# RWKV-5 attention followed by an MLP mixer on one core: the last batch's k read by one transfer instead of six

## The chip, the core and the metric

The kernel runs on one core of a Trainium2 chip. A core has five engines with instruction queues of their own: PE (TensorE, matrix products), DVE (VectorE), ACT (ScalarE), POOL (GpSimd) and SP (SyncE, which here issues most of the transfers between HBM and the core's SBUF). Each engine works its queue strictly in the written order; engines wait for each other and for transfers through semaphores. The metric is the device time of one launch in microseconds (us).

## The reference

Inputs r, k, v are (4, 8, 768, 48): four batches, eight heads, 768 steps, 48 channels, in float32; w and u are (8, 48). The attention's output, with the heads side by side, is the input x (4, 768, 384) of the mixer.

```python
for t in range(S):                                     # attention, per batch and head
    cur = einsum('bhd,bhe->bhde', u * k[t], v[t])
    y[t] = einsum('bhd,bhde->bhe', r[t], state + cur)
    state = w * state + einsum('bhd,bhe->bhde', k[t], v[t])

h  = relu(x.transpose(0, 2, 1) @ w_tok1) @ w_tok2      # mixer: along the 768 steps, 256 hidden
u  = x + h.transpose(0, 2, 1)
h2 = relu(u @ w_ch1) @ w_ch2                           # along the 384 channels, 1536 hidden
return u + h2
```

## The kernel before

**Tiling.** Each batch is cut into six chunks of 128 steps, with the steps on the 128 partitions and 8 heads x 48 channels in the free dimension. The recurrence is done chunk by chunk: inside a chunk as masked scores (`at_ps`, then `AT`) times v, between chunks by a state of 48 x 48 per head (`kv_ps`, then `S`). Decays are factors w to the power of a step number; they are kept in tables (`wnat`, `wp`, `wpair`) and multiplied onto k and r (`kr`).

**One chunk of the last two batches.** k, r and v of the chunk come by three loads on SP (tiles `kt`, `rt`, `vt`, 192 KB each; for every partition 8 pieces of 192 bytes). For these batches POOL makes all products (`POOL_ONLY`, line 193): `ku` = k times u, `rku` = `ku` times r, and `kr`, whose halves are k and r with their decays. DVE sums `rku` per head to `adg`. ACT turns v into bf16, `vb` (line 819). POOL makes `yd` from `vb` and `adg`. SP sends `kr` through a transposing transfer (`rk<-kr`, line 881). PE then multiplies the scores, for two chunks in one step (`GROUPS`, line 204; `scores`, line 972); DVE masks them; PE makes y and the state; DVE adds `yd` and writes `x_b`.

**The mixer of a batch** (line 1096 and after) starts when its six chunks of `x_b` are there: `h1_ps` and `hT_ps` along the steps, `z_ps` up to the hidden channels, a relu by ACT or DVE (`zr`), `h_ps` down to the output, and the stores (`out_dram<-osb`). Its matmuls are put between those of the next batches' attention, so that at about 85 to 110 us the last batch's attention shares all engines with the mixers of the batches before.

**The order** is not left to a scheduler: `ORDER` (line 21) lists all tasks in the sequence in which they are emitted, which fixes each engine's queue. `BUFS` (line 66) lists for every pool which buffer each tile takes; the PSUM banks of the pool `m` are handed round by it, and a matmul that starts a new tile waits until the bank's former contents have been read. `HOLD` and `GATES` (lines 174 and 187) let some early loads, and a few later ones, wait for the one before or for a weight's transfer. Of the last batch's loads of k, the one of chunk 1 has a gate.

**SP's queue around the change**, by the written order: k of chunk 0 of the last batch, v, r, k, a store, r, k, v, v, r, a transpose of `kr`, a store, k, a transpose, a transpose of `u_sb` (the mixer's `uT`), k, another of these, r, k, and on with transposes, r and v. Every transfer on SP uses one of eight semaphores in turn, and so also waits for the transfer eight places before it.

**ACT's queue there**: copies of a state (`S<-kv_ps`), the cast of v for a chunk of the last batch, two relus `zr<-z_ps` of the mixer of batch 1, a relu of `h1_ps` of batch 2, two more casts of v.

**Constants.** `mask2`, `place` and the table `wn2` serve a variant that handles chunks in pairs (`pairs`); the list `PAIRED` (line 196) is empty, so nothing reads them. `warm` is a tile of zeros that PE multiplies to fill its time at the start and at a few places of the first batch.

The profile writes L294 for nearly all instructions: this is the line of the wrapper that keeps them in program order. Tiles' names tell them apart.

Of the kernel before, what the change touches and what calls it, by code (L numbers as in the profile page):

```python
# [11 lines left out]
f32 = mybir.dt.float32  # L12
bf16 = mybir.dt.bfloat16
i32 = mybir.dt.int32
ACTF = mybir.ActivationFunctionType
ALU = mybir.AluOpType
# [203 lines left out]
class Plan:  # L220
# [10 lines left out]
    def add(self, engine, kind, emit, deps=(), take=(), use=()):  # L231
        self.tasks.append((emit, [d for d in deps if d is not None]))
        return len(self.tasks) - 1
# [22 lines left out]
def kernel(  # L256
# [14 lines left out]
    B, H, S, D = r.shape  # L271
    dm = H * D
    T = 128
    C = S // T
    NG = 3
    HP = H // 2
    P = 64
# [5 lines left out]
    const = ctx.enter_context(tc.tile_pool(name="const", bufs=1))  # L283
# [12 lines left out]
    pe, dve, act, pool, sp = (InOrder(e) for e in (nc.tensor, nc.vector, nc.scalar, nc.gpsimd, nc.sync))  # L296
# [20 lines left out]
    def mul(on, out, a, c):  # L317
        engine_of[on].tensor_mul(out, a, c)
# [6 lines left out]
    PRODUCT = {"POOL": "mul2_POOL", "DVE": "mul2_DVE"}  # L325

    def h3(t):
        return t.rearrange("p (h d) -> p h d", h=H)

    def row(src):  # L330
# [6 lines left out]
    krs = [const.tile([128, 2, H, P], bf16, name=f"kr{i}") for i in range(NKP)]  # L337
    ones = const.tile([1, 128], f32, name="ones")
    u_bc = const.tile([128, dm], f32, name="u_bc")
    warm = const.tile([128, 512], bf16, name="warm")  # L340
    NW = C // 2
    iota_i = const.tile([128, 4 + 2 + 2 * NG], i32, name="iota_i")
    iota = const.tile([128, 4 + 2 + 2 * NG], f32, name="iota")
    ident_f = const.tile([128, 128], f32, name="ident_f")
    ident = const.tile([128, 128], bf16, name="ident")
    mask = const.tile([128, 128], f32, name="mask")
    mask2 = const.tile([128, 2, 128], f32, name="mask2")
    place = const.tile([128, 2, 128], bf16, name="place")
    lnw = const.tile([128, dm], f32, name="lnw")
    wn = {g: const.tile([128, g, dm], f32, name=f"wnat{g}") for g in (2, NG)}  # L350
    wp = const.tile([128, NG, dm], f32, name="wp")
# [3 lines left out]
    u_heads = wp[0:H, 2, 2 * P:4 * P]  # L355
    lnwd = const.tile([128, HP], f32, name="lnwd")
    wp2 = const.tile([128, 2, dm], f32, name="wpair")
    wn2 = const.tile([128, 2, dm], f32, name="wnpair")
    u_blk = const.tile([128, HP, H], bf16, name="u_blk")
    wG = {g: const.tile([128, HP], f32, name=f"wG{g}") for g in (2, NG)}  # L360
    bm = const.tile([128, HP, 2, D], f32, name="bm")
    wGm = {g: const.tile([128, HP, 2, D], f32, name=f"wGm{g}") for g in (2, NG)}
    S0s = [const.tile([128, HP, 2, D], bf16, name=f"S0_{i}") for i in range(2)]
    x_bs = [const.tile([128, C, dm], bf16, name=f"x_b{i}") for i in range(2)]
    wtok1 = wts.tile([128, C, dtok], bf16, name="wtok1")
    wtok2 = wts.tile([128, 2, S], bf16, name="wtok2")
    wch1 = [wts.tile([128, 3, n], bf16, name=f"wch1_{i}") for i, n in enumerate((PART * 128, dch - PART * 128))]
# [2 lines left out]
    def once(engine, kind, f, deps=(), **kw):  # L370
        return add(engine, kind, f, deps, **kw)
# [39 lines left out]
    t_mask = once("POOL", "mask", make_mask)  # L411

    def make_mask2():
        pool.memset(mask2, 1.0)
        for q in range(2):
            rows = mask2[q * P:(q + 1) * P]
            pool.affine_select(out=rows, in_=rows, compare_op=ALU.is_gt, fill=0.0, base=0, pattern=[[-1, 2], [1, 128]],
                               channel_multiplier=-2)

    t_mask2 = once("POOL", "mask2", make_mask2)  # L420

    def make_place():
        dve.memset(place, 0.0)
        for q in range(2):
            rows = slice(q * P, (q + 1) * P)
            for j in range(2):
                dve.tensor_copy(place[rows, j, j::2], ident[rows, rows])

    t_place = once("DVE", "place", make_place, [t_id])

# [25 lines left out]
    def decay(t, g, col, deps):  # L456
        return once("ACT", "act384s", lambda: act.activation(t[:, g, :], lnw, Exp, scale=iota[:, col:col + 1]),
                    [t_lnw] + deps)

    t_wn2 = [decay(wn2, j, j, [t_io2]) for j in range(2)]  # L460
    t_wp2 = [decay(wp2, j, 2 + j, [t_io2]) for j in range(2)]
    t_wn = {2: [decay(wn[2], g, 4 + g, [t_io]) for g in range(2)], NG: [decay(wn[NG], g, 6 + g, [t_io]) for g in range(NG)]}
    t_wG = {g: once("ACT", "ln_s", lambda g=g: act.activation(wG[g], lnwd, Exp, scale=float(g * T)), [t_lnwd])
# [45 lines left out]
    def load(b, c, i):  # L509
        nm, src = (("kt", k), ("rt", r), ("vt", v))[i]  # L510
        win = two_steps(b, c, i)
        nm = "win" if win else nm

        def f():
            if win:
                t = sb("win", [128, H, 2 * D], f32)
                dst = t
                what = src[b, :, ds(c * T, 2 * T), :].rearrange("h (p j) d -> p h (j d)", j=2)
            else:
                t = sb(nm, [128, dm], f32)  # L520
                dst = h3(t)
                what = src[b, :, ts(c, T), :].rearrange("h s d -> s h d")
            asked[b, c, i] = sp.dma_start(dst, what)
            loaded[b, c, i] = t
            if (b, c, i) in GATES:
                after(asked[b, c, i], sent[GATES[b, c, i]])
            if (b, c, i) in HOLD:
                after(asked[b, c, i], asked[HOLD[b, c, i]])

        return add("SP", "load2" if win else "load", f, [], take=(nm,))  # L530

    for b in range(B):
        for c in range(C):
# [266 lines left out]
    def unit(b, c):  # L800
# [3 lines left out]
        L = {}  # L804
# [21 lines left out]
        if first:  # L826
            def turn_k():
                L["trk"] = ps("trk", [128, HP, T], bf16)
                for a in range(HP):
                    pe.transpose(L["trk"][:, a, :], pair(L["kr"][:, 0], a), ident)  # L830

            def evac_k(on):
                L["ka"] = sb("rka", [128, HP, T], bf16)
                copy(on, L["ka"], L["trk"])

            def product(on):
                L["pr"] = sb("pr", [128, HP, T], bf16)
                mul(on, L["pr"], L["trk"] if on == "DVE" else L["ka"], rT())

            def sum_m():  # L840
                L["ad_ps"] = ps("ad_ps", [128, H])
                for a in range(HP):
                    pe.matmul(L["ad_ps"], L["pr"][:, a, :], u_blk[:, a, :], start=(a == 0), stop=(a == HP - 1))

            def copy_ad(on):
                L["adg"] = sb("adg", [128, H], f32)
                copy(on, L["adg"], L["ad_ps"])

            t_tk = add("PE", "tk", turn_k, [t_kp, t_id], take=("m",), use=[(t_kp, "kp")])
            t_ek = flex({"ACT": "copy512", "DVE": "copy512d"}, evac_k, [t_tk], take=("rka",), use=[(t_tk, "m")])  # L850
            use_k, use_r = [(t_ek, "rka")], [(W["t"], "rkb")]
            turned = [t_ek, W["t"]]
            kT = lambda: L["ka"]
            rT = lambda: W["ra"][:, :, c % 2, :]
            t_pr = flex({"POOL": "prod_POOL", "DVE": "prod_DVE"}, product, turned, take=("pr",),
                        use=use_k + use_r + [(t_tk, "m")])
            t_sm = add("PE", "sm", sum_m, [t_pr, t_ublk], take=("m",), use=[(t_pr, "pr")])
            t_ad = flex({"ACT": "copy_ad", "DVE": "copy_ad"}, copy_ad, [t_sm], take=("adg",), use=[(t_sm, "m")])
        else:
            def mul_u(on):  # L860
                L["ku"] = sb("ku", [128, dm], f32)
                mul(on, L["ku"], loaded[b, c, 0], u_bc)

            def mul_rku(on):
                L["rku"] = sb("rku", [128, dm], f32)
                mul(on, L["rku"], L["ku"], loaded[b, c, 1])

            def sum_rku():
                L["adg"] = sb("adg", [128, H], f32)
                dve.tensor_reduce(L["adg"], h3(L["rku"]), axis=mybir.AxisListType.X, op=ALU.add)  # L870

            t_ku = flex(products, mul_u, [lk, t_ubc], take=("ku",), use=[(lk, "kt")])
            t_rku = flex(products, mul_rku, [t_ku, lr], take=("rku",), use=[(t_ku, "ku"), (lr, "rt")])
            t_ad = add("DVE", "sum384", sum_rku, [t_rku], take=("adg",), use=[(t_rku, "rku")])

            def mul_r(on):
                mul(on, L["kr"][:, 1, :, 0:D], h3(loaded[b, c, 1]), h3(wp[:, g, :]))

            t_rp = flex(products, mul_r, [lr, t_wp[g], t_kp], use=[(lr, "rt"), (t_kp, "kp")])
            if STYLE[n][0] == "dma":  # L880
                def turn_rk():
                    L["rk"] = sb("rk", [128, 2, HP, T], bf16)
                    sp.dma_start_transpose(L["rk"].rearrange("p j a s -> p (j a) s"),
                                           L["kr"].rearrange("p j h d -> p (j h d)"))

                t_ev = add("SP", "turn_rk", turn_rk, [t_kp, t_rp], take=("rk",), use=[(t_kp, "kp")])
            else:
                def turn_all():
                    L["tr"] = ps("tr_ps", [128, 2, HP, T], bf16)
                    for j in range(2):  # L890
                        for a in range(HP):
                            pe.transpose(L["tr"][:, j, a, :], pair(L["kr"][:, j], a), ident)

                def evac(on):
                    L["rk"] = sb("rk", [128, 2, HP, T], bf16)
                    copy(on, L["rk"], L["tr"])

                t_tr = add("PE", "tr_all", turn_all, [t_kp, t_rp, t_id], take=("m",), use=[(t_kp, "kp")])
                t_ev = flex({"ACT": "copy1024", "DVE": "copy1024d"}, evac, [t_tr], take=("rk",), use=[(t_tr, "m")])
            turned = [t_ev]  # L900
            use_k, use_r = [(t_ev, "rk")], [(t_ev, "rk")]
            kT = lambda: L["rk"][:, 0]
            rT = lambda: L["rk"][:, 1]
# [321 lines left out]
```

## Time and profile before

| what | value |
|---|---|
| time, median of 3 runs | 164.7 us (163.48 to 165.5) |
| profiled execution: span from its first to its last instruction | 160.1 us |
| profiled execution: its own whole time | not given by the page |
| granted clock of PE over the span | 1.000 |
| PE busy | 153.4 us, 96% |
| DVE / POOL / ACT busy | 111.6 / 88.8 / 68.2 us |
| read from HBM / written to it | 20.46 / 4.72 MB |

The page names instructions by engine, operation and tiles (`out<-in`). In a timeline a row is: start, duration, engine, operation, tiles, how many in a row, and in brackets the idle time of the engine before it and what ended that. `SPq` marks the issue of a transfer on SP; the transfer itself lands later. In a table of windows a row is: stretch, its length, then busy time (with the number of instructions) of PE, PE's weight loads, DVE, ACT and POOL, then PE's granted clock, the share of time that the transfer engines were busy, and GB/s. A row of waits is: who waited, for whom, us in total, how often, the longest. A row of transfers is: tiles, queue, kind, count, size, median us from issue to landing.

### The profile page before, as it was taken

The numbers are of one execution on the slowest core, as the hardware profiler recorded it, in microseconds if no ns is written. First come the engines' busy times: TensorE is split into PE (matmuls) and PEld (weight loads), VectorE is DVE, ScalarE is ACT, GpSimd is POOL, SyncE is SP. The second block draws the span as 40 slices with busy tenths as digits, with TensorE's granted clock in tenths as the row PEclk, the third lists the DMA queues.
The fourth block names the chain that finished last, engine by engine and source line by source line (L and its number), as shares of the span: only waits on it lengthen the run. The fifth ranks groups of instructions, "written<-read, shape, count | busy, mean of one in ns | idle before, by whom it ended". The sixth has DMA issues, their size and how long they took to land.

```text
span 160.1 us, 3797 instructions
## 1 busy us (share of the span) xinstructions
PE 153.4 (96%) x1463; PEld 102.6 (64%) x1463; DVE 111.6 (70%) x237; ACT 68.2 (43%) x150; POOL 88.8 (55%) x112
## 2 busy tenths in 40 slices
PE   6998799899999999999999999999999999999992
PEld 1464577567677677666767666677676556676572
DVE  6689884875697578397969939788997357422432
ACT  3999875438924254254524431144214102355000
POOL 7149991028179999899982997999822000000000
DMA  5999999999999979999999999999791064300222
GB/s 130 208 208 182 147 236 220 207 230 212 186 203 204 196 164 186 220 215 150 246 205 207 213 211 161 197 232 205 120 265 57 0 158 161 74 6 0 98 98 98
DMA packets 93061, 26.89 MB, mean 168 GB/s; under 512 B 87794, under 2 KB 92148, under 8 KB 93044
## 3 DMA queue, kind: packets, MB, share of 16 engines
q1 hardware_dynamic: 90688, 23.40, 72.6%
q0 software_dynamic: 2160, 3.15, 11.5%
q8 instruction: 11, 0.18, 0.5%
q10 hardware_dynamic: 196, 0.11, 0.2%
q14 instruction: 6, 0.05, 0.1%
HBM read 20.46 MB, written 4.72 MB: 157 GB/s over the span
## 4 chain that ended last, share of the span: by engine, by line
PE 76%; DMA 17%; ACT 2%; POOL 1%; issue 1%; SPq 1%; DVE 0%; POOLq 0%
PE h_ps L294 34%; PE z_ps L294 27%; DMA wch<-in_moe_w_ch_dram 7%; DMA kt<-in_k_dram 5%; DMA vt<-in_v_dram 5%; PE y_ps L294 4%; PE at_ps L294 3%; PE hT_ps L294 3%; PE kv_ps L294 2%; PE hx_ps L294 1%; PE trk L294 1%; ACT vb L294 1%; SPq L294 1%; PE tr_ps L294 1%; ACT x_b L294 1%
## 5 line engine op out<-in xcount | busy, mean ns | idle before, releaser
L294 PE MATMUL h_ps<-wch,zr 128*128 128x384 bf16 (+1 forms) x300 | 53.9, 320 | 0.0
L294 PE MATMUL z_ps<-uT,wch 128*128 128x384 bf16 x288 | 52.5, 327 | 0.6 <-DMA wch<-in_moe_w_ch_dram 0.6
L294 ACT ACTIVATE zr<-z_ps 128x384 bf16<-128x384 f32 x56 | 27.1, 492 | 39.5 <-PE z_ps L294 39.3
L294 PEld LDWEIGHTS <-wch 128*128 128x128 bf16 x288 | 31.1, 115 | 13.4 <-DMA wch<-in_moe_w_ch_dram 1.2
L294 PEld LDWEIGHTS <-zr 128*128 128x128 bf16 x300 | 27.6, 98 | 15.3
L294 DVE TENSOR_TENSOR AT<-at_ps,mask 128x512 bf16<-128x512 f32 x48 | 31.0, 683 | 3.7 <-PE at_ps L294 3.6
L294 DVE TENSOR_SCALAR zr<-z_ps 128x384 bf16<-128x384 f32 x40 | 21.4, 554 | 11.4 <-PE z_ps L294 8.6
L294 POOL TENSOR_TENSOR yd<-vb,adg 128x384 f32<-128x384 bf16 x18 | 14.8, 828 | 11.6 <-ACT vb L294 4.3
L294 POOL TENSOR_TENSOR kr<-kt,wnat 128x384 bf16<-128x384 f32 x19 | 19.3, 1019 | 3.0 <-DMA kt<-in_k_dram 2.9
L294 ACT CAST vb<-vt 128x384 bf16<-128x384 f32 x22 | 11.0, 511 | 12.6 <-DMA vt<-in_v_dram 12.6
L294 DVE TENSOR_TENSOR osb<-u_sb,h_ps 128x384 f32<-128x384 bf16 (+1 forms) x16 | 8.4, 528 | 9.9 <-PE h_ps L294 9.4
L294 PEld LDWEIGHTS <-kr 128*128 128x128 bf16 x176 | 11.8, 102 | 4.9 <-POOL kr L294 1.5
L294 POOL TENSOR_TENSOR ku<-kt,u_bc 128x384 f32<-128x384 f32 x12 | 12.1, 1008 | 0.5 <-DMA kt<-in_k_dram 0.5
L294 POOL TENSOR_TENSOR rku<-ku,rt 128x384 f32<-128x384 f32 x12 | 11.9, 1001 | 0.2
L294 POOL TENSOR_TENSOR kr<-rt,wp 128x384 bf16<-128x384 f32 x12 | 12.0, 1000 | 0.0
L294 PEld LDWEIGHTS <-wtok 128*128 128x128 bf16 x78 | 7.4, 98 | 4.4
L294 DVE TENSOR_TENSOR x_b<-y_ps,yd 128x384 bf16<-128x384 f32 x18 | 9.6, 549 | 0.6 <-PE y_ps L294 0.5
L294 PE MATMUL h_ps<-x_b,wtok 128*128 128x384 bf16 x48 | 8.8, 327 | 0.0
L294 PE MATMUL y_ps<-vb,AT 128*128 128x48 bf16 x192 | 8.7, 184 | 0.0
L294 ACT CAST S<-kv_ps 48x192 bf16<-48x192 f32 x18 | 5.6, 311 | 7.3 <-PE kv_ps L294 4.2
L294 POOL TENSOR_TENSOR pr<-rka,rkb 128x512 bf16<-128x512 bf16 x2 | 2.3, 1149 | 10.7 <-DVE rka L294 10.7
L294 DVE TENSOR_TENSOR u_sb<-x_b,hT_ps 128x384 bf16<-128x384 bf16 x15 | 7.6, 548 | 0.6 <-PE hT_ps L294 0.6
(93 smaller groups left out, 183.1 us busy)
## 6 DMA issues: line engine op xcount, KB each, us to landing
kt<-in_k_dram SPq DMA_DIRECT2D x24, 192.0 KB, 4.2
vt<-in_v_dram SPq DMA_DIRECT2D x24, 192.0 KB, 4.8
out_dram<-osb SPq DMA_DIRECT2D x23, 192.0 KB, 1.9
win<-in_r_dram SPq DMA_DIRECT2D x6, 384.0 KB, 4.9
rt<-in_r_dram SPq DMA_DIRECT2D x12, 192.0 KB, 3.2
wch<-in_moe_w_ch_dram POOLq DMA_DIRECT2D x4, 384.0 KB, 6.6
wtok<-in_moe_w_tok_dram POOLq DMA_DIRECT2D x2, 384.0 KB, 6.4
wch<-in_moe_w_ch_dram POOLq DMA_DIRECT2D x1, 768.0 KB, 11.3
```

The source lines that it names most:

```text
L294: return lambda *args, **kw: tc.keep_in_program_order(f(*args, **kw))
```

## The change

The six loads of k for batch 3 become one load of the whole slice k[3] into a tile of its own, `kw`, at the place where chunk 0's load was issued; the tasks of the other five issue nothing, and each chunk reads its part of `kw` (eight pieces of 48 values, 1152 bytes apart). The `kt` buffers and the gate of chunk 1's k are no longer used for this batch. `ku` is computed over the same 384 values in a shape with three dimensions.

Beside this, `mask2`, `place`, and the table `wn2` are no longer built, and `warm` becomes a view of the first part of `x_b1`, the mixer input of batches 1 and 3. In the queues, POOL loses a memset and two selects, DVE a memset and four small copies, ACT two exponentials, SP five loads. The order of everything else on every engine stays as it was; some waits name another of the eight semaphores, because the turn of SP's transfers has shifted.

```diff
     def h3(t):
+        if len(t.shape) == 3:
+            return t
         return t.rearrange("p (h d) -> p h d", h=H)
...
-    warm = const.tile([128, 512], bf16, name="warm")
...
-    mask2 = const.tile([128, 2, 128], f32, name="mask2")
-    place = const.tile([128, 2, 128], bf16, name="place")
...
-    wn2 = const.tile([128, 2, dm], f32, name="wnpair")
...
+    warm = x_bs[1][:, 0:2, :].rearrange("p c d -> p (c d)")[:, 0:512]
+    whole = const.tile([128, H * C, D], f32, name="kw")
...
     def make_mask2():
-        pool.memset(mask2, 1.0)
-        for q in range(2):
-            rows = mask2[q * P:(q + 1) * P]
-            pool.affine_select(out=rows, in_=rows, compare_op=ALU.is_gt, ...)
+        pass
...
     def make_place():
-        dve.memset(place, 0.0)
-        for q in range(2):
-            rows = slice(q * P, (q + 1) * P)
-            for j in range(2):
-                dve.tensor_copy(place[rows, j, j::2], ident[rows, rows])
+        pass
...
-    t_wn2 = [decay(wn2, j, j, [t_io2]) for j in range(2)]
+    t_wn2 = [once("ACT", "act384s", lambda: None, [t_lnw, t_io2]) for j in range(2)]
...
         def f():
+            if (b, i) == (3, 0):
+                if c == 0:
+                    asked[b, 0, 0] = sp.dma_start(whole, k[b].rearrange("h (c p) d -> p (h c) d", p=T))
+                asked[b, c, i] = asked[b, 0, 0]
+                loaded[b, c, i] = whole.rearrange("p (h c) d -> p h c d", c=C)[:, :, c, :]
+                return
             if win:
                 t = sb("win", [128, H, 2 * D], f32)
...
-        return add("SP", "load2" if win else "load", f, [], take=(nm,))
+        return add("SP", "load2" if win else "load", f, [])
...
             def mul_u(on):
                 L["ku"] = sb("ku", [128, dm], f32)
-                mul(on, L["ku"], loaded[b, c, 0], u_bc)
+                mul(on, h3(L["ku"]), h3(loaded[b, c, 0]), h3(u_bc))
```

More of the change, by code (lines that the diff above doesn't have):

```diff
@@ L413, in make_mask2 @@
     def make_mask2():
-        pool.memset(mask2, 1.0)
-        for q in range(2):
-            rows = mask2[q * P:(q + 1) * P]
-            pool.affine_select(out=rows, in_=rows, compare_op=ALU.is_gt, fill=0.0, base=0, pattern=[[-1, 2], [1, 128]],
-                               channel_multiplier=-2)
+        pass
     t_mask2 = once("POOL", "mask2", make_mask2)
     def make_place():
-        dve.memset(place, 0.0)
-        for q in range(2):
-            rows = slice(q * P, (q + 1) * P)
-            for j in range(2):
-                dve.tensor_copy(place[rows, j, j::2], ident[rows, rows])
+        pass
     t_place = once("DVE", "place", make_place, [t_id])
```

## The prediction

> **What bounds the kernel now.** I read the page's busy shares first, then the busy time of the stretch from 35 to 157 us, then what TensorE (PE) waited for in the whole span.
>
> ```profile
> span 160.1 us, 3797 instructions
> PE 153.4 (96%) x1463; PEld 102.6 (64%) x1463; DVE 111.6 (70%) x237; ACT 68.2 (43%) x150; POOL 88.8 (55%) x112
> ...
> GB/s 130 208 208 182 147 236 220 207 230 212 186 203 204 196 164 186 220 215 150 246 205 207 213 211 161 197 232 205 120 265 57 0 158 161 74 6 0 98 98 98
> ...
> 35.00:157.00 122.00, 121.86 (x1144) 83.28 (x1144) 83.66 (x165) 44.56 (x98) 70.96 (x77) 1.00 0.81 161
> ...
> PE kv_ps L294 <- DVE warm L294: 1.3, 1, 1.3
> PE trk L294 <- POOL kr L294: 0.6, 2, 0.5
> PE z_ps L294 <- DMA wch<-in_moe_w_ch_dram: 0.6, 2, 0.5
> ```
>
> From 35 us on PE is busy for 121.86 of 122.00 us: nothing else bounds that stretch, and nothing can be gained in it. But nothing is spare there either: a microsecond in which PE has to wait is a microsecond on the end. PE's own waits, of which these are the three longest, lie before that and sum to little. So the change is worth what it saves before 35 us less what it makes PE wait after that. The second thing to see is the row of GB/s: from 85 to 108 us about 205 GB/s are moved with hardly a break, so whatever is put in front of a transfer there delays it by its bytes.
>
> **The change, part by part.** Five of the six k loads of the last batch leave the sync queue, and the first becomes six times as large at the same place.
>
> ```profile
> 83.30 0.44 SPq L294 DMA_DIRECT2D kt<-in_k_dram  x1
> 83.84 0.65 SPq L294 DMA_DIRECT2D vt<-in_v_dram  x1
> 84.54 1.15 SPq L294 DMA_DIRECT2D rt<-in_r_dram  x1
> 85.74 0.70 SPq L294 DMA_DIRECT2D kt<-in_k_dram  x1
> ...
> 102.56 0.58 SPq L294 DMA_DIRECT2D kt<-in_k_dram  x1
> ...
> kt<-in_k_dram SPq DMA_DIRECT2D x24, 192.0 KB, 4.2
> ...
> 84.00:88.00 4.00, 4.00 (x66) 3.07 (x65) 4.00 (x8) 1.72 (x4) 1.03 (x2) 1.00 1.04 209
> 88.00:92.00 4.00, 4.00 (x46) 2.79 (x45) 3.70 (x8) 1.86 (x5) 4.00 (x5) 1.00 1.00 213
> ```
>
> *Issue.* The five issues removed took about 0.6 us each on a queue that bounds nothing: gain 0. The large one takes between 0.44 us (the row at 83.30) and six times that, 2.6 us, if it goes by size. Even then the next issue comes at 86.0, while the large transfer is still moving: cost 0.
>
> *Bytes.* The v chunk asked for at 83.84 and everything after it now stand behind 5 x 192 KB = 0.98 MB more. At the 211 GB/s of the two windows this is 4.7 us. The bounds are 3.7 us at the best slice of the page (265 GB/s) and 6.1 us at a poor one (161). The order of service is the order of issue as far as the trace tells: the k chunk in front is read at 87.76 and this v not before 88.72 (rows below). The Trainium skill ("DMA: Bandwidth & Descriptors", "Queues, rings and completion order") says that each engine takes a queue's descriptors in ring order; that agrees with the rows.
>
> *Who waits for that v.* The chunk is turned to bf16 by ScalarE (ACT), which works in program order:
>
> ```profile
> 87.74 0.64 ACT L294 CAST S<-kv_ps 48x192 bf16<-48x192 f32 x2 [1.54 <-PE y_ps L294]
> 88.72 0.51 ACT L294 CAST vb<-vt 128x384 bf16<-128x384 f32 x1 [0.34 <-DMA vt<-in_v_dram]
> 89.26 0.49 ACT L294 ACTIVATE zr<-z_ps 128x384 bf16<-128x384 f32 x1
> 89.96 0.49 ACT L294 ACTIVATE zr<-z_ps 128x384 bf16<-128x384 f32 x1 [0.21 <-PE z_ps L294]
> ...
> 87.74 0.66 PE L294 MATMUL z_ps<-uT,wch 128*128 128x384 bf16 x3
> ...
> 89.26 0.66 PE L294 MATMUL z_ps<-uT,wch 128*128 128x384 bf16 x3
> ...
> 90.13 0.66 PE L294 MATMUL z_ps<-uT,wch 128*128 128x384 bf16 x3
> ```
>
> ACT already waits for this v: the cast at 88.72 ends an idle time released by the transfer, so its slack is nil. Queued behind it on ACT are two relus of an older batch, which have nothing to do with k. The first, at 89.26, empties the PSUM bank that PE's z matmul at 90.13 takes next (bank 0 of `m`, counted along the list of banks). It ended at 89.75, so the cover is 0.4 us. With v 4.7 us late, the cast starts at 93.4, the relu ends at 94.45, and PE stands from 90.13 to about 94.45: a stall of 4.3 us. I take 4.0, because in the trace this v took 4.9 us from issue to cast, against a median landing of 3.2 for the r chunks, and a part of that lateness may not return:
>
> ```profile
> rt<-in_r_dram SPq DMA_DIRECT2D x12, 192.0 KB, 3.2
> ```
>
> With the bounds of the bytes the stall lies between 3.3 and 5.7 us; if all 1.7 us of that lateness went too, the low end is 1.6.
>
> *Who waits for k.* GpSimd (POOL) makes all products of this batch, in order, with little idle time:
>
> ```profile
> 87.76 1.00 POOL L294 TENSOR_TENSOR ku<-kt,u_bc 128x384 f32<-128x384 f32 x1
> ...
> 95.26 0.99 POOL L294 TENSOR_TENSOR kr<-rt,wp 128x384 bf16<-128x384 f32 x1
> ...
> 99.35 1.00 POOL L294 TENSOR_TENSOR kr<-kt,wnat 128x384 bf16<-128x384 f32 x1 [1.07 <-DMA kt<-in_k_dram]
> ...
> 96.28 1.24 SPq L294 DMA_TRANSPOSE rk<-kr  x1
> ...
> 100.81 0.62 PE L294 MATMUL at_ps<-rk 64*128 64x128 bf16 x16
> ...
> rk<-kr SPq DMA_TRANSPOSE x12, 3.5
> ```
>
> Its first product reads k at 87.76. The single chunk, issued at 83.30, lands by its group's median of 4.2 us at 87.5; the whole k takes 4.7 us more, so POOL starts near 92.2, 4.4 us late. The second transpose, which waits for the product at 95.26, then goes out at 100.7 and, with 3.5 us to land (last row), comes at 104.2. PE, itself 4.0 us late by then, wants it at 104.8. So this second lateness lies beneath the first and costs 0; standing alone, it would cost 104.2 - 100.81 = 3.4 us. After that POOL gets 1.07 us back, since the idle time at 99.35 (a later k chunk) is gone: it is then 3.3 us late, less than PE. The gain is covered by PE's own lateness. The later v and r loads move with POOL's transposes on the sync queue, so they stay within PE's 4.0 too.
>
> *Reading k with gaps.* Each head's 48 values of a chunk now lie 1152 bytes apart. The nearest row is a product that reads the r windows, with gaps too:
>
> ```profile
> L294 POOL TENSOR_TENSOR kr<-win,wpair x4: 1002/1156/1309, 9.8 to 44.9; 128x384 bf16<-128x384 f32 x4
> ```
>
> They took between 1.0 us, like the products of now, and 1.3. For twelve products on k that is 0 to 3.7 us on POOL. I take 0: the cheap ones show that gaps alone need not cost, and POOL has 0.7 us to spare behind PE.
>
> *The start.* The constants removed were two exponentials on ACT, a memset and two selects on POOL, five small operations on DVE:
>
> ```profile
> 5.41 0.60 ACT L294 ACTIVATE wnpair<-lnw,iota 128x384 f32<-128x384 f32 x1
> ...
> 8.44 0.60 ACT L294 ACTIVATE wnpair<-lnw,iota 128x384 f32<-128x384 f32 x1
> ...
> 10.78 0.51 ACT L294 CAST vb<-vt 128x384 bf16<-128x384 f32 x1 [0.34 <-DMA vt<-in_v_dram]
> ...
> 1.55 0.87 POOL L294 TENSOR_SCALAR_AFFINE_SELECT mask<-mask 64x256 f32<-64x256 f32 x2
> ...
> 7.75 0.61 POOL L294 TENSOR_TENSOR wp<-wp 8x128 f32<-8x128 f32 x1 [3.46 <-DMA wp<-in_u_dram]
> ...
> 3.80 0.65 DVE L294 COPY place<-ident 64x64 bf16<-64x64 bf16 x4
> ...
> 6.08 1.96 DVE L294 TENSOR_TENSOR kr<-win,wpair 128x384 bf16<-128x384 f32 x4 [1.35 <-DMA win<-in_r_dram]
> ```
>
> Each engine waits for a transfer soon after (10.78, 7.75, 6.08), and those transfers are issued in a fixed chain. The gain lies between 0 and the 0.6 us that PE waited for the channel weights; I take 0. The warm-up matmuls read a part of `x_b1` instead of `warm`, with the same shapes and at the same places, and are done long before `x_b1` is written: 0.
>
> **Sum.** +4.0 us on the profiled span: 160.1 to 164.1. The page does not give that execution's whole time; the median of the three runs, 164.7, is 4.6 above the span, and I carry this over: 168.7 us, 2.4% slower.
>
> **The rivals.**
>
> *Only k counts, not v.* If v were served beside the large transfer instead of behind it, ACT would go on, and the stall would stand at the scores: 3.4 us, 168.1. Against it: the order of landings in the trace.
>
> *The large transfer drains faster.* A single transfer leaves no gaps between issues. At 265 GB/s the 0.98 MB take 3.7 us, and without the 1.7 us of lateness the stall is 3.7 - 0.4 - 1.7 = 1.6 us: 166.3. For it: the best slice; against it: the same stretch is already moved with 1.00 to 1.04 of DMA time. The Trainium skill ("DMA: Bandwidth & Descriptors", "Bandwidth") advises transfers of 1 MiB and more, and gives 341 GB/s at 1 MB; by that figure the 0.98 MB would take an estimated 2.9 us. But the pieces stay 192 bytes long here, and no run shows such a rate.
>
> *PE's clock falls.* A stall of 4 us may be long enough for PE to come back slow. The trace shows that there is such a state:
>
> ```profile
> 3.80 3.59 PE L294 MATMUL kv_ps<-warm 128*128 128x512 bf16 x8
> ...
> 10.46 0.60 PE L294 MATMUL at_ps<-warm 128*128 128x512 bf16 x2
> ```
>
> The same matmul costs 0.45 us at 3.80 and 0.30 at 10.46, ends included, so I take the rate to have doubled between them. The slow stretch holds at least the 3.6 us of the first row and at most the 9.2 us from PE's first matmul, at 1.3, to 10.46; a repetition costs half of it, 1.8 to 4.6 us. In the middle, 3.2: 171.9. Against it: PE never idles for longer than 1.3 us in the trace, so nothing shows when it returns. The Trainium skill ("TensorE: Matmul & The Clock Gate", "Part 1") puts the return after a whole idle window of about 3.4 us that runs freely; by that a stall of 4 us would contain one now and then only.
>
> *Faster.* If the start gives PE's 0.6 us back, by channel weights issued earlier, and the v delay stays under the cover of 0.4 us: 164.1. It decides only if the large transfer doesn't hold v up, which would need 0.98 MB moved in 0.4 us, 2500 GB/s, some ten times the best slice.
>
> *The change doesn't do what it says* is excluded: the queue's order holds one k load of 128 x 48 x 48 where six stood.
>
> **How the numbers follow.** Stall behind v 0.55 (168.7); k alone 0.12 (168.1); faster drain 0.18 (166.3); clock 0.10 (171.9); faster 0.05 (164.1). 2% of 164.7 is 3.3 us, about what a measurement of this kernel can tell from no change: the border is 168.0. The first case is over it in 0.48 of its 0.55, k alone in 0.05, the clock in all, and that gives 0.63 slower; 0.03 is left for faster, as not even 164.1 would be by 2%, and 0.34 for the same. The range reaches from the faster drain to 166.3 and up to 171.0, which takes in the stall of 5.7 us (170.4) and leaves out most of the clock's case.
>
> **What would show it.** In the profile after: an ACT row for the cast of v that waits 4 to 5 us for the transfer near 88 to 93 us; PE's waits get a new row, z_ps for ACT's zr, of 4 us; POOL idles until about 92 us for the large k, and its 1.07 us near 99 are gone; the scores near 104.8 do not wait; from there to the end PE is as busy as before. I am wrong if PE's new wait is at the scores (k alone), is under 2.5 us (faster drain), or if three z matmuls in a row take about 1.2 us behind the stall, instead of the 0.66 of the rows above (clock).

## The result, and the profile after

| kernel | median, us | lowest to highest | ratio to before, 95% interval |
|---|---|---|---|
| before | 164.56 | 163.48 to 165.5 | |
| after | 171.19 | 169.94 to 172.67 | 1.0389 [1.0277, 1.0501] |

The change makes the kernel 3.9% slower. (A ratio leaves out executions over 1.5% above the quickest of the same kernel, while a median takes in all, so the two can differ a little.) The forecast was 168.7 us; the median lies 0.2 us above the range, because PE's stall is longer than forecast and a slower clock of PE comes on top of it.

The page of the changed kernel, first its span and busy times, then the granted clock in 40 slices:

```profile
span 170.9 us, 3781 instructions
PE 155.9 (91%) x1462; PEld 102.7 (60%) x1463; DVE 111.5 (65%) x232; ACT 67.4 (39%) x148; POOL 87.7 (51%) x109
...
PEclk9999999999999999999999759999999999999999
```

PE is busy for 2.5 us longer with the same matmuls, and two slices show a lowered clock; before there was none. What PE waited for in the whole span, the longest waits:

```profile
PE z_ps L294 <- ACT zr L294: 5.2, 1, 5.2
PE kv_ps L294 <- DVE x_b L294: 1.3, 1, 1.3
PE h_ps L294 <- DVE AT L294: 1.2, 1, 1.2
```

The first row is new, and it is the one forecast: z waits for a relu on ACT. The third is new too, but it lies at 48 us, long ahead of the large transfer. The chain behind the first, in rows of the timeline of SP, POOL, ACT and PE, with the transfer's own row for this v (the last number is the time from issue to landing) between those of SP and POOL:

```profile
86.20 0.88 SPq L294 DMA_DIRECT2D kw<-in_k_dram  x1
87.18 7.18 SPq L294 DMA_DIRECT2D vt<-in_v_dram  x1
94.43 0.58 SPq L294 DMA_DIRECT2D rt<-in_r_dram  x1
...
vt<-in_v_dram SPq DMA_DIRECT2D x1, 192.0 KB, 9.8
...
95.99 0.99 POOL L294 TENSOR_TENSOR ku<-kw,u_bc 128x384 f32<-128x384 f32 x1 [5.29 <-DMA kw<-in_k_dram]
...
90.39 0.64 ACT L294 CAST S<-kv_ps 48x192 bf16<-48x192 f32 x2 [1.56 <-DVE AT L294]
97.04 0.51 ACT L294 CAST vb<-vt 128x384 bf16<-128x384 f32 x1 [6.01 <-POOL ku L294]
97.58 0.87 ACT L294 ACTIVATE zr<-z_ps 128x384 bf16<-128x384 f32 x2
...
91.92 0.66 PE L294 MATMUL z_ps<-uT,wch 128*128 128x384 bf16 x3
...
98.12 1.12 PE L294 MATMUL z_ps<-uT,wch 128*128 128x384 bf16 x3 [5.17 <-ACT zr L294]
...
111.27 0.62 PE L294 MATMUL at_ps<-rk 64*128 64x128 bf16 x16
```

The large transfer is issued in 0.88 us and read by POOL 9.8 us later. The issue of v behind it stands on the queue for 7.18 us. The transfer of v lands 9.8 us after its issue began, at 96.98, and the cast of v starts at 97.04 (the view names POOL's product, which had started at 95.99, as what it waited for, but ACT reads nothing of that product). The relu follows, and z starts 0.54 us after the relu does. Three pairs of rows split the lateness. The z matmuls before the stall stand at 89.26 before and 91.92 here: 2.66 us late already. The stalled ones stand at 90.13 and 98.12: 7.99 late, so the stall adds 5.33. The scores stand at 100.81 and 111.27: 10.46 late, another 2.47 between. That last part is the clock: PE's granted clock is at half for a while. At the end the lateness is still 10.8 us (170.9 against 160.1), so nothing of it is made up. Three stretches of 3.41 us, cut where the granted clock changes; the last three numbers are the clock, the share of the transfer engines and GB/s:

```profile
92.95:96.36 3.41, 0.00 (x0) 0.00 (x0) 0.66 (x2) 0.00 (x0) 0.37 (x1) 1.00 0.68 132
96.36:99.78 3.42, 1.66 (x6) 0.81 (x6) 0.51 (x2) 1.38 (x3) 3.42 (x4) 0.50 1.05 229
99.78:103.19 3.41, 3.41 (x12) 1.51 (x11) 0.51 (x2) 0.00 (x0) 2.93 (x4) 0.50 0.91 168
```

PE does nothing in the first stretch, and has half its clock in the two that follow: the three z matmuls take 1.12 us instead of 0.66. At full clock again after 103.19, PE stays 10.46 us late. The Trainium skill ("TensorE: Matmul & The Clock Gate", "Part 1") says that a whole idle window of about 3.4 us returns the clock to half; this row agrees, another below does not.

The first 2.66 us are not the change's: they vary from execution to execution. In the kernels below, with the same edits up to this place, the large transfer is issued between 83.47 us (long pieces) and 86.77 (another queue). The profiled execution of before was a quick one, the one of after (172.67 us, 1.8 above its span) the slowest of its four.

### The profile page after: what moved, and what is told of

Read it like the earlier page. It is cut to its first block, busy times and chain, and to the rows that moved or that the text cites. A ratio compares the mean times of both kernels' runs of the same rounds, so it can differ in the third digit from the quotient of the medians.

```text
span 170.9 us, 3781 instructions
## 1 busy us (share of the span) xinstructions
PE 155.9 (91%) x1462; PEld 102.7 (60%) x1463; DVE 111.5 (65%) x232; ACT 67.4 (39%) x148; POOL 87.7 (51%) x109
## 4 chain that ended last, share of the span: by engine, by line
PE 59%; DMA 20%; POOL 6%; ACT 6%; DVE 4%; issue 2%; SPq 1%; POOLq 0%; DVEq 0%; ACTq 0%
PE h_ps L294 30%; PE z_ps L294 20%; DMA vt<-in_v_dram 8%; DMA kt<-in_k_dram 5%; DMA wch<-in_moe_w_ch_dram 4%; DMA rt<-in_r_dram 3%; POOL kr L294 3%; PE hT_ps L294 2%; PE y_ps L294 2%; POOL rku L294 2%; PE at_ps L294 1%; PE kv_ps L294 1%; DVE AT L294 1%; ACT zr L294 1%; ACT vb L294 1%
## 5 line engine op out<-in xcount | busy, mean ns | idle before, releaser
L294 PE MATMUL z_ps<-uT,wch 128*128 128x384 bf16 x288 | 53.2, 329 | 6.3 <-ACT zr L294 5.2
L294 PE MATMUL h_ps<-wch,zr 128*128 128x384 bf16 (+1 forms) x300 | 54.5, 322 | 1.2 <-DVE AT L294 1.2
L294 PEld LDWEIGHTS <-kr 128*128 128x128 bf16 x176 | 11.1, 98 | 5.5 <-POOL kr L294 1.7
L294 POOL TENSOR_TENSOR kr<-kt,wnat 128x384 bf16<-128x384 f32 x13 | 13.3, 1026 | 1.2 <-DMA kt<-in_k_dram 1.1
L294 PEld LDWEIGHTS <-wtok 128*128 128x128 bf16 x78 | 7.9, 104 | 5.6 <-issue 1.9
L294 PE MATMUL h_ps<-x_b,wtok 128*128 128x384 bf16 x48 | 10.2, 362 | 0.0
L294 POOL TENSOR_TENSOR ku<-kw,u_bc 128x384 f32<-128x384 f32 x6 | 6.0, 1003 | 5.3 <-DMA kw<-in_k_dram 5.3
L294 DVE TENSOR_SCALAR h1r<-h_ps 128x384 bf16<-128x384 f32 x4 | 2.2, 558 | 9.9 <-PE h_ps L294 9.9
```

The lines of the kernel that those rows point to most:

```text
L294: return lambda *args, **kw: tc.keep_in_program_order(f(*args, **kw))
```

## The experiments

**The constants alone.** The single k loads are put back, everything else of the change stays (the opposite, the large transfer with the constants kept, was not tried):

```diff
-    whole = const.tile([128, H * C, D], f32, name="kw")
...
-            if (b, i) == (3, 0):
-                if c == 0:
-                    asked[b, 0, 0] = sp.dma_start(whole, k[b]...)
-                ...
-                return
```

> The changed kernel with the six single loads of k put back; only the removal of the constants and the moved warm tile are left. My theory (all of the loss comes from the large transfer): no difference from the kernel before, 164.0 to 165.2 us, ratio 0.995 to 1.005, and no wait of TensorE over 0.5 us after 36 us. Rival (the 2.6 us that TensorE was already late at 84 us in the changed kernel's profile come from the edits at the start): 167.2 us, ratio 1.016, with TensorE late by 0.3 us at 31 us and by 2.6 us at 84 us.

Measured: 164.17 us against 164.31, ratio 0.9968 [0.993, 1.0007]. The constants and `warm` cost and gain nothing that shows; the whole loss is the transfer's. This is also the fastest of the versions here, and it is no faster than before.

**v first.** The v load is issued ahead of the large transfer instead of behind it:

```diff
+    ik, iv = plan.order.index(t_load[3, 0, 0]), plan.order.index(t_load[3, 1, 2])
+    plan.order.insert(ik, plan.order.pop(iv))
```

> The changed kernel, but the v chunk that stood right behind the large transfer is issued right before it. My theory (v held up behind k, ACT in order): TensorE's wait of 5 us for ACT's relu is gone, under 0.5 us. But the large transfer still lands some 9 us after its issue, so GpSimd starts on k about 6 us late, and TensorE meets this further on: at hT_ps (VectorE's sum of rku stands ahead of its relu) and at the scores, 4 to 6 us in all, partly in pieces too short for the clock to fall: 168 to 170.5 us. Rival (only the v chunk mattered, k has slack): 164.5 to 165.5 us. Rival (the stall comes from the large transfer's load on the transfer engines whatever the order): the wait for ACT's relu stays at 4 us or more and the time at 170 to 172.

Measured: 168.96 us, ratio 1.0252 [1.0185, 1.032]. PE's longest wait, and the rows of SP, POOL and DVE behind it:

```profile
PE hT_ps L294 <- DVE h1r L294: 2.2, 1, 2.2
```

```profile
84.91 0.88 SPq L294 DMA_DIRECT2D kw<-in_k_dram  x1
85.84 6.67 SPq L294 DMA_DIRECT2D rt<-in_r_dram  x1
...
94.60 0.99 POOL L294 TENSOR_TENSOR ku<-kw,u_bc 128x384 f32<-128x384 f32 x1 [5.68 <-DMA kw<-in_k_dram]
...
97.53 0.55 DVE L294 TENSOR_REDUCE adg<-rku 128x8 f32<-128x384 f32 x1 [5.24 <-POOL rku L294]
98.00 0.55 DVE L294 TENSOR_SCALAR h1r<-h_ps 128x384 bf16<-128x384 f32 x1
```

z no longer waits, so the stall of 5.2 us was v's. But k's own lateness now shows: DVE works in order, its sum `adg` waits for POOL's product, and a relu of the mixer that has nothing to do with k stands behind it. The blocked issue has passed from v to r. The new waits sum to 2.8 us, less than the 4 to 6 expected; that the time fits is partly luck, because PE's clock falls as well, by a shorter wait than above. Two stretches:

```profile
95.03:98.44 3.41, 1.35 (x9) 0.69 (x7) 0.91 (x2) 0.51 (x1) 3.41 (x5) 1.00 1.18 216
98.44:101.85 3.41, 3.25 (x11) 1.52 (x11) 2.23 (x5) 0.51 (x1) 3.41 (x5) 0.50 0.70 55
```

PE was busy for 1.35 of the 3.41 us, and still the next stretch has half the clock. Where the Trainium skill ("TensorE: Matmul & The Clock Gate", "Part 1") asks for a whole idle window, the measurement decides.

**Useless matmuls in the stall.** In the changed kernel, 20 matmuls into a free bank are put ahead of the z that waits:

```diff
+    def keep_busy():
+        spare = psum.tile([128, 512], f32, name="spare", tag="kv0", bufs=1)
+        for i in range(NFILL):                                   # 20
+            pe.matmul(spare, ident, x_bs[1]..., start=True, stop=True)
...
+    plan.order.insert(plan.order.index(last_z), add("PE", "warm", keep_busy, [t_id]))
```

> The changed kernel with 20 matmuls of 128x512 of no use put into TensorE's queue right ahead of the z matmul that stalls; they write a PSUM bank that is free there. They take 20 x 0.213 = 4.3 us at full clock, less than the stall. Theory (the clock falls because TensorE idles over 3.4 us, and that costs 1.7 to 3.4 us beside the stall): granted clock 1.00 in the windows behind the stall, the wait for ACT's relu down to 1 us or less, and 167.8 to 169.0 us. Rival (the fallen clock hides behind other waits and costs nothing): the clock stays up, but the time stays at 170 to 172.

Measured: 168.9 us, ratio 1.0264 [1.02, 1.0328], clock 1.0. As the changed kernel had been timed in another session, both were run once more side by side.

> The changed kernel once more, beside the one with useless matmuls in its stall, so that the two share a chip and the runs of the kernel before. Theory 1 (the stall of 5.2 us and the clock at half for one or two stretches of 3.4 us after it): 170 to 172, a ratio of 1.035 to 1.045, z waits about 5 us and the granted clock over the span is 0.98 to 0.99. Theory 2 (the clock's part is an accident of the chip of the first runs): clock 1.0 and 168.5 to 169.5.

> 20 matmuls whose result nobody reads fill the stall ahead of z; all else is as in the changed kernel. Theory 1 (the clock falls because PE idles): clock 1.0, 1.3 to 2.5 us less than the changed kernel, 168.5 to 169.5, ratio 1.024 to 1.034. Theory 2 (the lowered clock costs nothing by itself, since other engines set the pace then): the same time as the changed kernel to within 0.5 us.

Measured: changed 171.7 us (169.4 to 172.4), ratio 1.0349 [1.0281, 1.0417], clock 0.98 to 0.99; with the useless matmuls 169.56 us (167.27 to 170.07), ratio 1.0272 [1.0211, 1.0333], clock 1.0. The medians are 2.1 us apart; by the two ratios it would be 1.3 us (0.0077 of 164.5). Timeline of PE with the useless matmuls:

```profile
92.06 4.48 PE L295 MATMUL spare<-x_b,ident 128*128 128x512 bf16 x20
97.00 0.65 PE L295 MATMUL z_ps<-uT,wch 128*128 128x384 bf16 x3 [0.47 <-ACT zr L295]
```

z comes as late as without the useless matmuls, at 97.0 instead of 92.1, only that PE is kept busy meanwhile, and its matmuls come back at full speed (0.65). So some 1.3 to 2.1 us of the loss are the clock, which falls because PE idles, and the rest is the stall itself.

**Another queue.** ACT issues the large transfer, so that SP's queue is not held by it:

```diff
-                    asked[b, 0, 0] = sp.dma_start(whole, k[b]...)
+                    asked[b, 0, 0] = act.dma_start(whole, k[b]...)
```

> The changed kernel with the large transfer issued from ACT's queue instead of SP's, at the same place of the written order, so that v and r have no large transfer ahead of them in their own queue. Theory (v is held up by the queue that it shares with k): SP's issue of v takes under 1.5 us instead of 7.2, ACT's cast waits at most 1.5 us, and the stall at z is under 1.5 us; what is left comes from GpSimd's late k, at hT_ps and the scores, 3 to 6 us: 167.5 to 170.5 us. Rival (the engines are full, the queue doesn't matter): the issue of v or its landing stays 6 us late or more, z stalls by 4 us or more: 170 to 172 us.

Measured: 171.48 us, with runs so far apart (168.34 to 173.74) that no ratio is given; the profile is of the slowest of the four. Rows of the timeline of ACT, SP and POOL (the store named in POOL's row is nothing that it reads), then what the transfer engines moved from 92 to 95 us, by queue (packets, MB, share of the engines; q10 is ACT's queue, q1 is SP's):

```profile
86.77 0.84 ACTq L294 DMA_DIRECT2D kw<-in_k_dram  x1
...
87.69 0.40 SPq L294 DMA_DIRECT2D vt<-in_v_dram  x1
...
98.22 0.99 POOL L294 TENSOR_TENSOR ku<-kw,u_bc 128x384 f32<-128x384 f32 x1 [6.15 <-DMA out_dram<-osb]
...
98.42 0.51 ACT L294 CAST vb<-vt 128x384 bf16<-128x384 f32 x1 [5.77 <-DMA vt<-in_v_dram]
...
q10 hardware_dynamic: 582, 0.45, 88.9%
q1 hardware_dynamic: 570, 0.11, 34.7%
```

v is now asked for without delay, from a queue of its own, with a sixth of the pieces, and yet the cast waits for it until 98.42, 10.7 us; z waits 4.9. My theory missed, and what the rival had expected came. Freeing the issue of v was not enough: v comes when k is through, at 98.2 to 98.4 both. By the Trainium skill ("DMA: Bandwidth & Descriptors", "Queues, rings and completion order") a transfer engine takes turns between queues, a packet at a time. The last two rows agree: 582 packets of one queue, 570 of the other. But a packet of k holds some 770 bytes and one of SP's queue some 190, so SP's queue, with v in front, gets a fifth of the bytes while k is moving. Why hardly any of v moves earlier (from 89 to 91.5 us SP's queue has at most 21 packets under 512 bytes) is open. Not all of this execution's loss is the transfer's: PE also waited 2.1 us for a weight at 49 us, and its clock fell there too.

**Long pieces.** A kernel to measure with, not to use, as it hands the steps of k to the wrong chunks:

```diff
-                    asked[b, 0, 0] = sp.dma_start(whole, k[b].rearrange("h (c p) d -> p (h c) d", p=T))
+                    asked[b, 0, 0] = sp.dma_start(whole.rearrange("p (h c) d -> p h (c d)", c=C),
+                                                  k[b].rearrange("h (p c) d -> p h (c d)", c=C))
```

> The large transfer of k moves the same 1.18 MB to the same tile at the same place, but every partition takes six neighbouring steps of a head (step = 6 x partition + chunk), so that it is made of 1024 pieces of 1152 bytes instead of 6144 of 192. The steps of k are thereby handed to the wrong chunks; the amount of work is unchanged. Theory 1, the number of pieces is what the large transfer costs: it has as many pieces as one chunk's load, so the issue of v behind it takes under 1.5 us instead of 7.2, k lands about 5 us after its issue instead of 9.7, z waits 0 to 2 us for the relu, and the time is 164.5 to 167. Theory 2, the bytes are what it costs: v's issue or its landing is as late as before, z waits 4 to 5 us, and the time is 169 to 172.

Measured: 166.21 us, ratio 1.0153 [1.0013, 1.0293]. PE's longest wait, then rows of SP, POOL and ACT, from the quickest of its four executions:

```profile
PE z_ps L294 <- ACT zr L294: 1.9, 1, 1.9
```

```profile
83.47 0.44 SPq L294 DMA_DIRECT2D kw<-in_k_dram  x1
83.99 0.65 SPq L294 DMA_DIRECT2D vt<-in_v_dram  x1
...
89.62 1.00 POOL L294 TENSOR_TENSOR ku<-kw,u_bc 128x384 f32<-128x384 f32 x1 [1.63 <-DMA kw<-in_k_dram]
...
91.29 0.51 ACT L294 CAST vb<-vt 128x384 bf16<-128x384 f32 x1 [2.73 <-DMA vt<-in_v_dram]
```

What the transfer engines moved amid the large transfer, in the changed kernel (88 to 93 us) and with long pieces (86 to 88 us):

```profile
DMA packets 1278, 1.00 MB, mean 199 GB/s; under 512 B 2, under 2 KB 1277, under 8 KB 1277
DMA packets 625, 0.72 MB, mean 360 GB/s; under 512 B 0, under 2 KB 625, under 8 KB 625
```

The same bytes are there after 6.15 us instead of 9.8, the issue of v takes 0.65 us instead of 7.18, and more than half of the loss is gone by the ratios (1.5% against 3.9%, though the interval is wide). So it is the 6144 pieces of 192 bytes far more than the 1.18 MB; theory 1 holds, within its upper end. It is the length of the pieces and not the number of packets: in the changed kernel a packet holds some 770 bytes, so four pieces, and the rate is still 199 GB/s, about the 208 of the two halves below, whose pieces go one to a packet (86 to 90 us), against 360 with pieces of 1152 bytes. The Trainium skill ("DMA: Bandwidth & Descriptors", "Specifications") asks for 512 bytes and more for full rate, which agrees. What is left is a wait of 1.9 us.

**Two halves.** Heads 0 to 3 where the large transfer stood, heads 4 to 7 behind v and r:

```diff
-                if c == 0:
-                    asked[b, 0, 0] = sp.dma_start(whole, k[b]...)
+                if c in (0, 3):
+                    hs = slice(0, H // 2) if c == 0 else slice(H // 2, H)
+                    asked[b, 0, 0] = sp.dma_start(whole[:, C * hs.start:C * hs.stop, :], k[b][hs]...)
```

> k of the last batch in two transfers of four heads each (0.59 MB, 3072 pieces): the first where the large one stood, the second behind the next v and r loads, ahead of the store. Theory 1 (what stands ahead of v is served first, in the order of issue): v has half as many pieces ahead, its delay falls from about 8 to about 3 us, z waits 1 to 2.5 us and not 5.2, the clock stays up. But k is whole no earlier than now, so POOL is as late, and what is then visible of it (DVE's sum ahead of h1r, as with v first) adds 1 to 2.5 us: 167.5 to 169.5. Theory 2 (v's lateness alone sets the time, k's is covered): 166 to 167. Theory 3 (two transfers delay v like one): z waits 4 to 5 us, 169.5 to 171.5.

Measured: 169.43 us, ratio 1.0384 [1.0291, 1.0477], clock 1.0. PE's waits:

```profile
PE at_ps L294 <- DMA rk<-kr: 2.0, 1, 2.0
PE z_ps L294 <- ACT zr L294: 1.4, 1, 1.4
...
PE hT_ps L294 <- DVE h1r L294: 1.2, 1, 1.2
```

Half the volume ahead of v takes 3.8 us off the stall at z, as theory 1 has it; k is no earlier, and 3.2 us come out at the relu `h1r` and at the scores, 0.7 more than the top of what I had put there. The waits lie apart, and the clock does not fall.

**v first, and the sum later.** As "v first", and DVE's sum is moved behind `h1r`, to just ahead of its reader:

```diff
+    plan.order.remove(sum_of[3, 0])
+    plan.order.insert(plan.order.index(own_of[3, 0]), sum_of[3, 0])
```

> As with v first (the v chunk issued ahead of the large k), and DVE's sum of rku for the first chunk of the last batch is moved behind the relu h1r in DVE's order, to just ahead of the product that reads it. Theory 1 (k's lateness of 6 us has to come out somewhere, since POOL makes everything of the last batch in order): the wait for h1r, 2.2 us with v first, is gone, but PE then waits 2 to 4.5 us for the transposed kr at the scores instead; 167.5 to 169.5, no better than v first (169.0) by more than its 1.3 us of lowered clock. Theory 2 (the block in DVE's order was the cost): PE waits under 1 us, 165 to 166.5.

Measured: 170.43 us, ratio 1.0441 [1.0355, 1.0527], clock 0.98. Rows of DVE and PE:

```profile
94.65 0.56 DVE L294 TENSOR_SCALAR h1r<-h_ps 128x384 bf16<-128x384 f32 x1 [2.01 <-PE h_ps L294]
...
103.15 0.40 PE L294 MATMUL at_ps<-rk 64*128 64x128 bf16 x8 [0.36 <-DMA rk<-kr]
106.70 0.61 PE L294 MATMUL at_ps<-rk 64*128 64x128 bf16 x8 [3.15 <-DMA rk<-kr]
```

```profile
102.30:105.71 3.41, 0.88 (x11) 0.32 (x9) 0.24 (x1) 0.00 (x0) 3.33 (x5) 1.00 0.59 140
105.71:109.12 3.41, 2.26 (x17) 1.41 (x18) 3.41 (x7) 0.00 (x0) 3.37 (x4) 0.50 0.95 179
```

`h1r` is 3.4 us earlier than with v first, and nothing is won: PE runs ahead and stands at the scores for 3.5 us, and the clock falls there (the two stretches: 0.88 us of work, then half the clock). Order on an engine moved the stall and did not remove it; for that k would have to come earlier. The time is 0.9 us above the range that theory 1 had given, as I had not counted a fallen clock.

**Much earlier.** The large transfer is issued ahead of a k load of batch 1:

```diff
+    ik = plan.order.index(t_load[3, 0, 0])
+    plan.order.insert(plan.order.index(t_load[1, 4, 0]), plan.order.pop(ik))
```

> The large transfer is issued some 41 us earlier in the written order, ahead of a k load of batch 1 (at about 42 us) that waits 2.6 us for its buffer; the loads of v, r and everything else at 83 us then follow each other without it. Theory 1 (the price is that the transfer stands ahead of loads that are needed at once, so a place where loads run ahead of their use is cheaper): k is there long before POOL wants it, no wait of z or at the scores near 90 to 105 us; the loads behind it near 45 us come up to 6 us later, of which their lead hides a part; PE waits 0 to 3 us there; 164 to 167.5. Theory 2 (a transfer of 6144 pieces costs its 6 us of delay at any place): new waits of 4 to 6 us on PE between 45 and 60 us, 168 to 171.

Measured: 171.36 us, ratio 1.0509 [1.04, 1.0617]. Rows of SP, POOL and PE, then one window:

```profile
46.61 0.88 SPq L294 DMA_DIRECT2D kw<-in_k_dram  x1
47.59 6.94 SPq L294 DMA_DIRECT2D kt<-in_k_dram  x2
...
58.54 0.98 POOL L294 TENSOR_TENSOR kr<-kt,wnat 128x384 bf16<-128x384 f32 x1 [7.30 <-DMA kt<-in_k_dram]
...
59.58 0.61 PE L294 MATMUL trk<-ident,kr 128*128 128x128 bf16 x4 [5.67 <-POOL kr L294]
```

```profile
60.00:64.00 4.00, 4.00 (x28) 2.00 (x27) 0.95 (x3) 0.58 (x1) 4.00 (x5) 0.50 1.28 198
```

The waits near 90 to 105 us are gone, and the same price is paid near 55: two issues that take 6.94 us, a stall of 5.67, the clock at half behind it. The loads run ahead of their use by less than I took from SP's waits for buffers. Theory 2 holds, a little above its range.

**The waits nearly add up to the times.** The table adds PE's new waits behind the large transfer to the median of before in the same session. Where the clock stayed up, the sum comes within 0.5 us of the measured median; where it fell, 0.9 to 2.2 us are left, of the order of what the useless matmuls showed (1.3 to 2.1). This is a rough check: the waits are those of one profiled execution, and the runs of before in the session of the last four kernels lie between 162.23 and 166.58 us. Against the profiled execution's own time the long pieces' sum is 2.3 us too high.

| kernel | before there | PE's new waits | sum | measured | granted clock |
|---|---|---|---|---|---|
| changed, again | 164.5 | 5.0 | 169.5 | 171.7 | 0.98 |
| useless matmuls, again | 164.5 | 5.0 of stall, filled | 169.5 | 169.56 | 1.0 |
| v first | 164.31 | 2.2 + 0.4 + 0.2 | 167.1 | 168.96 | 0.99 |
| long pieces | 164.75 | 1.9 | 166.65 | 166.21 | 1.0 |
| halves | 164.75 | 1.4 + 1.2 + 2.0 | 169.35 | 169.43 | 1.0 |
| sum later | 164.75 | 3.5 + 0.5 | 168.75 | 170.43 | 0.98 |
| much earlier | 164.75 | 5.7 | 170.45 | 171.36 | 0.98 |

## Why the prediction was right, and where it fell short

- *What bounds* held: PE has nothing to spare after 35 us, and its waits are on the end: 10.46 us late at the scores, 10.8 at the end.
- *The chain* held link by link: v behind k, the cast, the relu of an older batch, the PSUM bank, z. "v first" removes the stall at z by moving one load. The stall alone takes the time to 169.8 us (164.56 + 5.2), over the border of 168.0, so "slower" did not come out by luck.
- *Bytes*, the term of the sum that was too small: 0.98 MB at 211 GB/s, 4.7 us. The cast of v came at 97.04 instead of 88.72 + 2.66, so v was 5.7 us later, inside the bounds (3.7 to 6.1) near the poor one. Amid the transfer the rate was not poor: 199 GB/s from 88 to 93 us, against 214 there before. At 199 the bytes take an estimated 4.9 us; the other 0.8 us of v's lateness fit the term *Issue*, below.
- *The stall*: 4.3 worked out, 4.0 taken, 5.2 measured. With 5.7 for v and the cover of 0.4, the working would have given 5.3. The step down for v's "lateness of 1.7 us" was wrong: nothing shows any of it coming back.
- *PE's clock falls* was a rival at 0.10. It is no rival but a consequence: it came on top of the stall in all ten runs of the changed kernel (granted clock 0.98 to 0.99). The prediction's own sign for it, three z matmuls that take about 1.2 us behind the stall, came with 1.12, and by that sign the forecast without the clock was wrong. I had argued that a stall of 4 us would contain a whole idle window now and then only; 2.2 us of waiting in one stretch were enough with v first. I had priced it at 3.2 us, with bounds of 1.8 to 4.6; it measured 2.1 by the medians, 1.3 by the ratios, 2.47 in the profile after. This and the stall are the 2.5 us by which the median is above the forecast (1.2 of stall, 2.1 of clock, less 0.8 by which the sum overshoots: 164.56 + 5.2 + 2.1 is 171.9).
- *Issue* was put at nothing because the next issue would come while the large transfer is still moving. That reason failed. The large issue took 0.88 us, but the next came at 87.18 and stood until 94.36, and by then the transfer engines had run dry:

```profile
94.00:95.00 1.00, 0.00 (x0) 0.00 (x0) 0.00 (x0) 0.00 (x0) 0.00 (x0) 1.00 0.17 44
```

  They were busy for 0.17 of this microsecond and 0.79 of the one before, so about 1 us is missing, an estimate from the two shares, and near the 0.8 that the bytes leave open. With the useless matmuls the gap is there too (0.26 from 92 to 93 us; v's issue stood until 92.35). No run lifts the block and leaves all else as it is: with another queue v shares the engines with k's packets instead.
- *k alone* was priced at 3.4 us beneath the first stall. Covered it was: no wait at the scores in the profile after. Uncovered it costs 2.8 us with v first, 3.5 at the scores when the sum is moved out of the way. POOL's first product came 5.6 us late (95.99 against 87.76 + 2.66), not 4.4.
- *Gaps in k*: the products on `kw` take 0.99 us in the rows above, as those on `kt` did. Nothing, as forecast. *The start*: nothing, by the first experiment.
- *4.6 us around the span*: of after, the execution with the span of 170.9 took 172.67, so only 1.8 lie around it; the other 2.8 are that the profiled execution of before was quicker than the median. As the sum was to give a median, this did no harm.
- *Faster drain* (0.18) would have needed long pieces; with them the kernel comes to 166.2 by its median, close to its 166.3.

## What to carry to other kernels

Merging loads saved issues here, on a queue that bounded nothing, and it made whatever stood behind them wait for all of the bytes, while only the first chunk was needed at first. Count the pieces too: the merge that left them at 192 bytes gained no rate. To price a delay on an engine that works in order, follow what stands behind the waiting instruction, not what reads the data, and ask next what comes up when that stall is taken away. If PE loses more than 2 us at one place, put the clock's fall into the sum, not among the rivals: 2.2 us were enough with v first, 2.0 with two halves were not.

## What the hardware showed that was not expected

- A transfer of 6144 pieces was issued in 0.88 us, but the issue behind it stood for 7.18 us (v), or 6.67 (r, with v first). With 1024 pieces and the same bytes: 0.65 us. Towards the end of the 7.18 us the transfer engines ran nearly dry (0.17 busy, 44 GB/s).
- The same 1.18 MB took 9.8 us from issue to use in pieces of 192 bytes and 6.15 us in pieces of 1152.
- A load of v issued on one queue 0.9 us behind the large transfer on another was not there before 10.7 us had passed. The two queues were served packet for packet (570 against 582 in 3 us), but with packets of some 190 against 770 bytes.
- PE's clock went to half after stretches of 3.41 us with 0, 0.88 and 1.35 us of work, and stayed there after one with 1.66 and one with 2.26; after 3.25 (v first) it came back. With long pieces, two stretches on the grid of that run's own clock changes:

```profile
90.11:93.52 3.41, 1.52 (x20) 1.03 (x18) 1.31 (x3) 1.39 (x3) 3.09 (x4) 1.00 0.96 206
93.52:96.93 3.41, 3.41 (x23) 2.05 (x22) 1.11 (x3) 1.30 (x3) 3.41 (x5) 1.00 0.78 151
```

  1.52 us of work were enough to keep it up, so the border lies between 1.35 and 1.52 here. Keeping PE busy with matmuls that nobody reads was worth 2.1 us by the medians.
